# Expert weight splits queued behind the latest hidden-block eviction

## Chip, cores and metric

The kernel runs on one core of a Trainium2 chip. The metric is the device time of one execution in microseconds (us); the figure given for a kernel is the median of several runs.

## The reference

Three stages follow each other: attention with capped scores, a dense two-layer block, and a mixture of eight experts in which every token goes to one expert and every expert takes 224 tokens.

```python
scores = cap * tanh(scale * q @ k.T / cap); attn = softmax(scores)   # 4 x 12 heads, 448 x 64
x = attn @ v                                    # as 1792 tokens x 768
g = relu(x @ w_in) ** 2; x = g @ w_out          # 768 -> 2048 -> 768
logits = x @ w_gate                             # 8 experts
# pairs (token, expert) in falling order of logit; a pair is taken if the
# token is free and the expert has fewer than 1792 / 8 = 224 tokens
for e in range(8):
    out[mask_e] = relu(x[mask_e] @ w1[e]) @ w2[e]   # 768 -> 1024 -> 768, float32
```

## The kernel before

TensorE multiplies in a one-pass 32-bit format that keeps fewer bits than float32. To hold float32 accuracy an operand is split in a high part (a copy in the short format) and a low part (the rest), and three products are summed: high by high, high by low, low by high. For a weight tile of 128 x 768 the split is one copy on ScalarE (L361) and one subtraction on VectorE (L362, called the low half here), in `split_weights`.

The experts run one after the other (`experts`, `expert`). Each has 16 weight tiles, 8 of `w1` and 8 of `w2`, used in that order. This document counts them through: number 16 k + j is tile j of `w1` of expert k, 16 k + 8 + j that of `w2`. In the first half of an expert, block j multiplies the 224 gathered tokens with tile j of `w1` into a PSUM accumulator `acc` (two buffers; in expert 0 some blocks use a `big` one), and is then evicted: ScalarE applies relu and writes the high part (L884), VectorE computes relu again less the high part (L885). The evicted blocks `g` are the stationary operand of the second half, which multiplies them with the tiles of `w2` into two `big` accumulators (L935), copied out (L911) and scattered to the output by POOL (L913). The first four experts multiply their first half in float32 without a split (L867); experts 4 to 7 use split tiles (L874). So 96 of the 128 tiles are split.

A weight tile is loaded by SP's queue (L834) into one of the buffers `wf` (3), `raw` (3) or `g` (6 of a pool of 16), in a pattern that repeats every 12 numbers. `load_experts(n)`, called when tile n is asked for, states loads up to number n + 12 and splits up to number n + 4. The split's results lie in `wh` and `wl`, eight buffers of each in two pools. Before a tile can be loaded the expert that it belongs to must be known: the routing, which picks the experts' tokens with many small VectorE steps (L618 to L768) and small matmuls (L676 to L761), runs beside the experts, and so does the feeding of the next expert: POOL gathers its rows (L783), TensorE transposes them (L802), ScalarE and VectorE split them (L809, L810).

The order of instructions on each engine is fixed when the program is built. On TensorE it is written out. On the other engines a planner plays the program through on an estimated time line: at each point an engine takes, of the instructions that are ready by that estimate, the one of best priority. Priority is the order of statement; `high_priority(5000)` puts the evictions and the feeding ahead of all that is not marked, `high_priority(2000)` the routing. On the chip each engine then works its queue in that order. `issue_after(ins)` gives the planner an edge: the instructions stated in its block on the engine of `ins` take a place behind `ins` in that engine's queue. It adds no wait between engines. Before the change only one such edge concerns the splits: those of expert 0 come behind the latest routing step `self.picks` on VectorE.

Of the kernel before, what the change touches and what calls it, by code (L numbers as in the profile page):

```python
# [9 lines left out]
F32 = mybir.dt.float32  # L10
# [5 lines left out]
AF = mybir.ActivationFunctionType  # L16
OP = mybir.AluOpType
# [14 lines left out]
NF2 = F2 // 128  # L32
# [53 lines left out]
class Kernel:  # L86
# [50 lines left out]
    def second(self, room):  # L137

        self.te, self.late = 0.0, 0
        self.stored = 0  # L140
        self.side = [[0.0, chain(self.last_logits(), self.routes())]]

        def then():
            room()
            yield 0.0

        e = chain(self.output(NB - 1), then(), self.output(LAST), self.experts())
        stuck = False
        while True:
            s = min(self.side, key=lambda x: x[0], default=None)  # L150
            if s is not None and (s[0] <= self.te or stuck):
                stuck = False
                self.te = max(self.te, s[0])
                try:
                    with self.tc.high_priority(2000):
                        wait, pe = next(s[1])
                    s[0] = max(s[0], self.te - 0.5) + wait + pe
                    self.te += pe
                except StopIteration:
                    self.side.remove(s)  # L160
                continue
            try:
                step = next(e)
            except StopIteration:
                return
            stuck = step is None
            self.te += step or 0.0
# [675 lines left out]

    def split_expert(self):
        if len(self.ew[self.eready]) > 1:
            with self.tc.issue_after(self.picks.ins) if self.eready < 2 * NF2 else nullcontext():
                self.ew[self.eready] = self.split_weights(*self.ew[self.eready])

    def expert(self, k):
        nc, ep = self.nc, self.ep  # L850
        xs, idx = self.xe[k], self.rows[k][2]
        hT = []
        W, H = {}, {}

        def part(j, d0, d1):
            if d0 == 0:
                W[j] = [t.rearrange("p (d f) -> p d f", d=ND) for t in self.expert_weights(k, 1, j)]
                if k == 0 and 2 <= j < EARLY:
                    if j % 2 == 0:
                        big = self.psum.tile([128, 2, 512], F32, name="big")  # L860
                        for i in range(2):
                            H[j + i] = big[:, i, :CAP]
                else:
                    H[j] = self.psum.tile([128, CAP], F32, name="acc")
            if k < PLAIN:
                for d in range(d0, d1):
                    nc.tensor.matmul(H[j], W[j][0][:, d], xs[:, d, 0].bitcast(F32), start=(d == 0), stop=(d == ND - 1))  # L867
                    if d % 2:
                        yield 0.8
                return  # L870
            wh, wl = W[j]
            for d in range(d0, d1):
                for w, x, first, last in ((wh, 0, True, False), (wh, 1, False, False), (wl, 0, False, True)):
                    nc.tensor.matmul(H[j], w[:, d], xs[:, d, x], start=(d == 0 and first), stop=(d == ND - 1 and last))  # L874
                if d % 2:
                    yield 0.6

        def evict(j):
            ps = H.pop(j)
            if j % 2 == 0:  # L880
                W["pair"] = self.mp.tile([128, 2, S], F32R, name="g", bufs=NF)
            hT.append(W["pair"][:, j % 2].rearrange("p (a c) -> p a c", a=2))
            with self.tc.high_priority(5000):
                nc.scalar.activation(hT[j][:, 0], ps, AF.Relu)  # L884
                nc.vector.scalar_tensor_tensor(hT[j][:, 1], ps, 0.0, hT[j][:, 0].bitcast(F32), op0=OP.max, op1=OP.subtract)  # L885

        if k == 0:
            for i in range(EARLY):
                p = part(i, 0, DA)
                if i == 0:  # L890
                    yield next(p)
                    yield from self.trailing()
                yield from p
            while self.gathered == 0:
                yield None
            yield from self.feed(0, 1)
        groups = ((0,), (1,), (2, 3), (4, 5), (6,), (7,)) if k == 0 else [(j,) for j in range(NF2)]
        for group in groups:
            for j in group:
                yield from part(j, DA if k == 0 and j < EARLY else 0, ND)  # L900
            for j in group:
                evict(j)
        acc = [self.psum.tile([TP, 2, 512], F32, name="big") for _ in range(2)]
        turned = None

        def store(h):
            if h:
                o = ep.tile([TP, 2, DM // 2], F32, name="o", bufs=1)
            else:
                o = self.mp.tile([128, 2 * S], F32, name="lt", bufs=1)[:TP, :DM].rearrange("p (a b) -> p a b", a=2)  # L910
            nc.scalar.copy(o, acc[h][:, :, :DM // 2])  # L911
            nc.gpsimd.memset(self.spacer, 0.0)
            st = nc.gpsimd.indirect_dma_start(  # L913
                out=self.out, out_offset=bass.IndirectOffsetOnAxis(ap=idx[h][:, :1], axis=0),
                in_=o.rearrange("p a b -> p (a b)"), in_offset=None)
            for s in self.scatters:
                self.tc.declare_no_dep(st.ins, s.ins, reason="rows of other tokens")
            self.scatters.append(st)

        both = [(j, h) for j in range(NF2) for h in range(2)]  # L920
        if k == NE - 1:
            both = both[:NF2] + [(j, h) for h in range(2) for j in range(NF2 // 2, NF2)]
        W2 = {}
        for j, h in both:
            if j >= NF2 // 2 and h == 0 and k + 1 not in self.xe and k + 1 < self.gathered:
                turned = chain(self.feed(k + 1, 0), self.feed(k + 1, 1))
            if j not in W2:
                W2[j] = self.expert_weights(k, 2, j)
            wh, wl = W2[j]
            if turned is not None:  # L930
                yield next(turned, 0.0)
            a, z = (hT[j][:, i, h * TP:(h + 1) * TP] for i in range(2))
            for l, r, first, last in ((a, wh, True, False), (a, wl, False, False), (z, wh, False, True)):
                for s in range(2):
                    nc.tensor.matmul(acc[h][:, s, :DM // 2], l, r[:, s * (DM // 2):(s + 1) * (DM // 2)],  # L935
                                     start=(j == 0 and first), stop=(j == NF2 - 1 and last))
                yield 0.325
            if j == NF2 - 1:
                if h and turned is not None:
                    yield from turned  # L940
                store(h)
        yield 0.5
# [56 lines left out]
```

## Time and profile before

| | |
|---|---|
| median of 3 runs | 1073.3 us (1072.6 to 1077.36) |
| the profiled execution, its own time | 1071.56 us |
| its span, first to last instruction | 1069.8 us |
| TensorE busy | 1034.6 us, 97% |
| VectorE, ScalarE, POOL busy | 604.1, 470.4, 246.6 us |
| mean granted TensorE clock | 0.991 |
| DMA | 237.60 MB, mean 222 GB/s |

Busy time is the time in which an engine had an instruction in work; the ends of matmuls are modelled. A clock of 1.00 is 2.4 GHz and 0.50 is 1.2 GHz. Times in the rows below are counted from the start of the span. In a timeline row the bracket at the end gives the engine's idle time before the instruction and what ended it by the semaphores; no bracket means no idle time worth a note.

### The profile page before, as it was taken

To read this page: it belongs to the slowest core of one execution; us is meant where nothing else is said; L and a number is where in the kernel's file an instruction comes from. 1 tells how busy PE (TensorE), PEld (TensorE's weight loads), DVE (VectorE), ACT (ScalarE), POOL (GpSimd) and SP (SyncE) were. 2 spreads that over 40 slices of the span, in tenths; PEclk is the share of its full clock that TensorE was granted. 3 is DMA by queue.
4 is the path that set the end of the run, shared out by engine and by line. 5 is a ranking of instruction groups with operands and counts; after the bars stand their busy time and mean duration, and the time that the engine had idled before them with its cause. 6 is when DMAs were issued, how large, how long until landed. Compare 5 with 4: busy or idle time off the path is not lost.

```text
span 1069.8 us, 15661 instructions
## 1 busy us (share of the span) xinstructions
PE 1034.6 (97%) x5690; PEld 817.9 (76%) x5690; DVE 604.1 (56%) x1148; ACT 470.4 (44%) x725; POOL 246.6 (23%) x181
## 2 busy tenths in 40 slices
PE   6989999999999999999999999999999999989997
PEld 1335655777777777777888888888899989989997
DVE  5997999998222156566311234453655456666551
ACT  5867686644555633465534110112242233444551
POOL 0117785675221232221000100002220201021000
PEclk8999999999999999999999999999999999999998
DMA  8644777799655589987885368667663539555620
GB/s 277 225 171 134 255 267 261 239 325 334 234 184 182 162 282 348 381 276 272 289 296 192 117 195 278 200 197 231 235 243 133 175 135 321 163 180 185 203 80 27
DMA packets 102495, 237.60 MB, mean 222 GB/s; under 512 B 11089, under 2 KB 21873, under 8 KB 102417
## 3 DMA queue, kind: packets, MB, share of 16 engines
q1 hardware_dynamic: 87776, 219.65, 60.6%
q0 software_dynamic: 3424, 11.19, 3.4%
q10 hardware_dynamic: 11216, 5.75, 2.0%
q8 instruction: 45, 0.74, 0.3%
q14 instruction: 34, 0.27, 0.1%
HBM read 194.08 MB, written 42.47 MB: 221 GB/s over the span
## 4 chain that ended last, share of the span: by engine, by line
PE 67%; issue 13%; DVE 11%; DMA 4%; ACT 2%; POOL 1%; SPq 0%; POOLq 0%; ACTq 0%; DVEq 0%
PE big L935 8%; PE acc L404 7%; PE acc L405 6%; PE acc L406 6%; PE acc L461 6%; PE acc L462 6%; PE acc L463 6%; PE aux L263 4%; PE acc L867 4%; PE big L239 3%; DVE wf L334 3%; DVE wf L333 2%; PE acc L874 2%; PE aux L676 2%; DVE wf L335 1%
## 5 line engine op out<-in xcount | busy, mean ns | idle before, releaser
L461 PE MATMUL acc<-g,wh 128*128 128x448 f32 x384 | 149.5, 389 | 0.0
L404 PE MATMUL acc<-xh,wh 128*128 128x448 f32 x384 | 146.0, 382 | 0.8 <-ACT r L411 0.8
L405 PE MATMUL acc<-xl,wh 128*128 128x448 f32 x384 | 141.2, 368 | 0.5 <-DVE xl L321 0.5
L462 PE MATMUL acc<-g,wh 128*128 128x448 f32 x384 | 140.1, 365 | 0.0
L406 PE MATMUL acc<-xh,wl 128*128 128x448 f32 x384 | 139.9, 364 | 0.0
L463 PE MATMUL acc<-g,wl 128*128 128x448 f32 x384 | 139.6, 364 | 0.0
L935 PE MATMUL big<-wh,g 128*112 128x384 f32 x512 | 118.5, 342 | 1.5 <-DVE g L885 1.5
L243 ACT ACTIVATE p<-big,isc 128x896 f32<-128x896 f32 x96 | 85.8, 907 | 45.0 <-PE big L239 44.2
L272 DVE RECIPROCAL z<-z 128x448 f32<-128x448 f32 x24 | 70.8, 2949 | 57.4 <-ACT z L271 57.3
L416 DVE TENSOR_TENSOR g<-r,g 128x448 fp32r<-128x448 f32 x58 | 42.7, 737 | 104.4 <-ACT g L415 104.1
L404 PEld LDWEIGHTS acc<-xh,wh 128*128 128x128 f32 x384 | 71.6, 187 | 34.2 <-issue 16.3
L244 ACT ACTIVATE p<-p,capt 128x896 f32<-128x896 f32 x96 | 89.3, 948 | 1.7
L783 POOL DMA_INDIRECT xg<-x,idx x32 | 30.8, 964 | 255.4 <-PE aux L676 129.6
L935 PEld LDWEIGHTS big<-wh,g 128*112 128x112 f32 x512 | 86.6, 175 | 2.4 <-DVE g L885 1.8
L461 PEld LDWEIGHTS acc<-g,wh 128*128 128x128 f32 x384 | 73.2, 191 | 11.7 <-issue 5.6
L263 PE MATMUL aux<-p,v 128*64 128x448 f32 x384 | 81.2, 549 | 0.4 <-DVE z L271 0.3
L405 PEld LDWEIGHTS acc<-xl,wh 128*128 128x128 f32 x384 | 72.4, 189 | 10.0 <-DVE xl L321 2.5
L239 PE MATMUL big<-qk 64*128 64x448 f32 x288 | 73.5, 600 | 6.7 <-DMA qk<-qk 6.4
L361 ACT CAST wh<-wf 128x768 fp32r<-128x768 f32 (+1 forms) x64 | 47.9, 751 | 72.9 <-DMA wf<-w 17.3
L411 ACT ACTIVATE r<-acc 128x448 f32<-128x448 f32 x64 | 34.8, 543 | 99.1 <-PE acc L406 87.6
L406 PEld LDWEIGHTS acc<-xh,wl 128*128 128x128 f32 x384 | 72.3, 188 | 6.8 <-issue 0.8
L462 PEld LDWEIGHTS acc<-g,wh 128*128 128x128 f32 x384 | 72.4, 189 | 6.3 <-issue 2.2
(179 smaller groups left out, 1841.2 us busy)
## 6 DMA issues: line engine op xcount, KB each, us to landing
g<-w SPq DMA_DIRECT2D x62, 384.0 KB
wh<-wih SPq DMA_DIRECT2D x48, 384.0 KB
wl<-wil SPq DMA_DIRECT2D x48, 384.0 KB
wh<-woh SPq DMA_DIRECT2D x72, 256.0 KB
wl<-wol SPq DMA_DIRECT2D x72, 256.0 KB
wf<-w SPq DMA_DIRECT2D x33, 384.0 KB
raw<-w SPq DMA_DIRECT2D x33, 384.0 KB
raw<-w_in SPq DMA_DIRECT2D x16, 768.0 KB
```

Source lines behind the costliest of these rows:

```text
L239: nc.tensor.matmul(ps[:, s, :S], k[rows], q[rows], start=True, stop=True)
L243: nc.scalar.activation(p, ps[:, :n, :S], AF.Tanh, scale=self.isc)
L244: e = nc.scalar.activation(p, p, AF.Exp, scale=self.capt)
L263: nc.tensor.matmul(U[hp][s * 64:s * 64 + 64], vt[hp][:, c, s * 64:s * 64 + 64], P[hp, c][:, s if c < KB else 0], start=(c == 0), stop=(c = ...
L272: nc.vector.reciprocal(d, d)
L404: nc.tensor.matmul(ps, wh[:, d], xh, start=(d == 0), stop=False)
L405: nc.tensor.matmul(ps, wh[:, d], xl, start=False, stop=False)
L406: nc.tensor.matmul(ps, wl[:, d], xh, start=False, stop=(d == ND - 1))
L461: nc.tensor.matmul(ps, a, gh, start=(f == 0), stop=False)
L462: nc.tensor.matmul(ps, a, gl, start=False, stop=False)
L463: nc.tensor.matmul(ps, z, gh, start=False, stop=(f == NF - 1))
L935: nc.tensor.matmul(acc[h][:, s, :DM // 2], l, r[:, s * (DM // 2):(s + 1) * (DM // 2)], start=(j == 0 and first), stop=(j == NF2 - 1 and last))
```

## The change

`expert` keeps the two instructions of the eviction stated last in `self.evicts`, and `split_expert` states each split with two more edges: the copy on ScalarE takes a place behind that eviction's ScalarE instruction, the low half behind its VectorE instruction. Until the first eviction of expert 0 is stated there is nothing to come behind. Number, kind and size of the instructions stay as they are.

```diff
@@ second
-        self.stored = 0
+        self.stored, self.evicts = 0, None
@@ split_expert
         if len(self.ew[self.eready]) > 1:
-            with self.tc.issue_after(self.picks.ins) if self.eready < 2 * NF2 else nullcontext():
+            with self.tc.issue_after(self.picks.ins) if self.eready < 2 * NF2 else nullcontext(), self.behind(0), self.behind(1):
                 self.ew[self.eready] = self.split_weights(*self.ew[self.eready])
+
+    def behind(self, i):
+
+        return self.tc.issue_after(self.evicts[i].ins) if self.evicts else nullcontext()
@@ expert, evict
             with self.tc.high_priority(5000):
-                nc.scalar.activation(hT[j][:, 0], ps, AF.Relu)
-                nc.vector.scalar_tensor_tensor(hT[j][:, 1], ps, 0.0, hT[j][:, 0].bitcast(F32), op0=OP.max, op1=OP.subtract)
+                self.evicts = (nc.scalar.activation(hT[j][:, 0], ps, AF.Relu),
+                               nc.vector.scalar_tensor_tensor(hT[j][:, 1], ps, 0.0, hT[j][:, 0].bitcast(F32), op0=OP.max, op1=OP.subtract))
```

## Rows read from the trace of the kernel before

**Rows 1.** The page, busy us (share of the span) xinstructions.

```profile
PE 1034.6 (97%) x5690; PEld 817.9 (76%) x5690; DVE 604.1 (56%) x1148; ACT 470.4 (44%) x725; POOL 246.6 (23%) x181
```

**Rows 2.** Waits of TensorE and ScalarE, 840 to 1070: us in total, times, longest.

```profile
PE acc L867 <- DVE g L885: 2.9, 3, 2.1
...
PE acc L874 <- DVE g L885: 1.6, 4, 0.9
...
ACT wh L361 <- PE acc L874: 33.3, 30, 2.1
```

**Rows 3.** Timeline of TensorE: start, us, instruction, xcount [idle before <-releaser].

```profile
767.88 0.61 PE L935 MATMUL big<-wh,g 128*112 128x384 f32 x2 [1.46 <-DVE g L885]
...
878.10 5.12 PE L867 MATMUL acc<-xs,raw 128*128 128x224 f32 x24 [2.07 <-DVE g L885]
...
892.50 0.68 PE L935 MATMUL big<-wh,g 128*112 128x384 f32 x2
...
912.46 0.46 PE L874 MATMUL acc<-xs,wh 128*128 128x224 f32 x2
...
957.93 0.48 PE L874 MATMUL acc<-xs,wh 128*128 128x224 f32 x2 [2.64 <-issue]
```

**Rows 4.** Timeline of ScalarE.

```profile
764.13 0.83 ACT L361 CAST wh<-wf 128x768 fp32r<-128x768 f32 x1 [1.78 <-DMA wf<-w]
764.87 0.35 ACT L884 ACTIVATE g<-big 128x224 fp32r<-128x224 f32 x1
...
875.78 0.83 ACT L361 CAST wh<-wf 128x768 fp32r<-128x768 f32 x1 [4.00 <-DMA wf<-w]
876.51 0.35 ACT L884 ACTIVATE g<-acc 128x224 fp32r<-128x224 f32 x1
...
914.63 0.84 ACT L361 CAST wh<-wf 128x768 fp32r<-128x768 f32 x1 [0.49 <-PE acc L874]
...
954.40 0.83 ACT L361 CAST wh<-raw 128x768 fp32r<-128x768 f32 x1 [2.89 <-PE aux L709]
955.14 0.35 ACT L884 ACTIVATE g<-acc 128x224 fp32r<-128x224 f32 x1
```

**Rows 5.** Timeline of VectorE.

```profile
876.64 0.96 DVE L362 TENSOR_TENSOR wl<-wf,wh 128x768 fp32r<-128x768 f32 x1 [1.98 <-ACT wh L361]
...
877.66 0.39 DVE L885 SCALAR_TENSOR_TENSOR g<-acc,g 128x224 fp32r<-128x224 f32 x1
...
955.83 0.39 DVE L716 TENSOR_TENSOR A<-aux,room 128x224 bf16<-128x224 f32 x1 [3.06 <-PE acc L874]
956.14 0.38 DVE L718 TENSOR_TENSOR V<-aux,base 128x224 f32<-128x224 f32 x1
956.44 0.27 DVE L717 TENSOR_TENSOR A<-A,tm 128x224 bf16<-128x224 bf16 x1
956.62 0.95 DVE L362 TENSOR_TENSOR wl<-raw,wh 128x768 fp32r<-128x768 f32 x1
957.49 0.39 DVE L885 SCALAR_TENSOR_TENSOR g<-acc,g 128x224 fp32r<-128x224 f32 x1
```

**Rows 6.** Stretches: us, busy PE, PEld, DVE, ACT, POOL, clock, DMA share, GB/s.

```profile
871.00:893.00 22.00, 19.07 (x112) 17.44 (x111) 14.12 (x57) 5.57 (x12) 2.08 (x3) 1.00 0.64 210
893.00:913.00 20.00, 20.00 (x136) 18.86 (x136) 12.32 (x29) 8.64 (x13) 2.20 (x3) 1.00 0.86 304
...
951.00:975.00 24.00, 20.44 (x157) 19.76 (x157) 15.06 (x40) 9.23 (x17) 4.68 (x5) 0.93 0.66 213
```

**Rows 7.** Timeline of SP, loads of weights, merged by buffer kind.

```profile
871.41 6.54 SPq L834 DMA_DIRECT2D wf<-w  x3
...
889.17 1.91 SPq L834 DMA_DIRECT2D wf<-w  x3
```

**Rows 8.** Timeline of VectorE and TensorE, feeding of expert 5.

```profile
942.39 0.60 DVE L810 TENSOR_TENSOR xs<-acc,xs 128x448 fp32r<-128x448 f32 x1
...
943.05 0.60 PE L802 MATMUL acc<-cf,xg 112*128 112x112 f32 x4 [0.17 <-DVE xs L810]
```

## The prediction

> **What bounds the kernel now.** I read four views in this order. First the page's busy times: TensorE is busy 1034.6 us, 97% of the span [rows 1], so a change that leaves the matmuls alone can only take out TensorE's idle time and its time at the lower clock. Before the expert stage (about 740 us) the edited function orders nothing, so the question is how much idle time is left behind that point and what ends it. Second, the waits and the timeline of TensorE: behind 740 us the idle time that ends with an eviction on VectorE (L885, the second half of a hidden block's eviction) is 1.46 us at 767.88 in expert 0, 2.9 us in three waits in expert 3 (the longest, 2.07 us, ends at 878.10) and 1.6 us in four waits in experts 4 to 6; 2.64 us more, which the profile puts down to "issue", end at 957.93 in expert 5 [rows 2, 3]. Third, what stood ahead of these evictions. On ScalarE, expert 3: the split (L361) of a `wf` weight sat at the head of the queue for 4.00 us until its load landed, ran from 875.78 for 0.83 us, and only then came the eviction L884 at 876.51 [rows 4]. On VectorE the low half of that split began at 876.64 and the eviction's half L885 at 877.66, ending 878.05 [rows 5]; TensorE went on at 878.10. So a ready eviction stood behind a split that waited for a load. Expert 0 has the same picture: the split at 764.13 waited 1.78 us for its load, the eviction followed at 764.87 [rows 4]. Fourth, the 2.64 us in expert 5 are no "issue": the engine resumed at 957.93, 0.05 us after the eviction's half that ran 0.39 us from 957.49 [rows 3, 5]. Ahead of that one VectorE worked A (L716, 955.83), two routing steps and a low half (956.62, 0.95 us), and on ScalarE a split at 954.40 stood ahead of the eviction at 955.14 [rows 4, 5].
>
> **The change part by part.** No instruction is added, removed or resized; each split's copy and low half get a place in their queues behind the eviction stated last. Splits are stated four weights ahead of their use but run up to eight ahead now: 30 of them in the stretch behind 840 us wait only until TensorE has released the buffer that they write [rows 2]. That release is the end of a block's matmuls, the very moment at which that block's eviction becomes ready, and the split, stated for a weight eight later, is first in the queue. Behind the change a split stated in block j has to follow the eviction of block j-1, so between two evictions stands the one split stated there and not the one eight ahead; splits stated in the second half of an expert, or in the first block of the next, follow only the last eviction of the expert in work.
>
> Step 1, expert 0: the splits of its second half, numbers 12 to 15, move behind eviction 7, and 10 and 11 behind 5 and 6. The 1.46 us go. What is late next: split 10 is needed by the third weight of the second half, and its copy and low half cost 0.83 + 0.96 us [rows 4, 5], on engines that were idle waiting for that load. Taken as 1.46 gained (bounds 0 and 1.46).
>
> Step 2, expert 3: numbers 60 to 63 move behind the eviction of block 7. All three waits go: 2.9 us. What is late next: the four come due together at the start of the second half, now at 892.50, then about 889.6. Four copies are 3.3 us on ScalarE, four low halves 3.8 us on VectorE. The second half takes 892.50 to 912.46, 20.0 us for eight weights [rows 3], 2.5 each; the first of the four is its fifth weight, 10 us in, so there are 6 us to spare. Cover gone, a late one costs its lateness, at most 3.8 us. VectorE in that stretch is busy 12.3 of 20 us [rows 6]: four low halves come in and three (69 to 71, held behind evictions of expert 4) go out, 13.3. Taken as 2.9 (bounds -0.9 and 2.9).
>
> Step 3, experts 4 to 7, every block: the eviction no longer stands behind 0.83 us of copy and 0.96 us of low half, and has those 1.8 us more until its accumulator is wanted two blocks on. Waits of 1.6 us in four cases are all shorter than 1.8 (the longest 0.9 [rows 2]), so I take the whole 1.6 (bounds 0 and 1.6).
>
> Step 4, expert 5: ScalarE's eviction can run at 954.40 in place of the split. On VectorE A waits for its matmul until 955.83 and I leave it ahead; the eviction follows it directly at about 956.2, in place of two routing steps (0.3 us and 0.2 us, from their starts [rows 5]) and the low half (0.95, overlapping by 0.1). It ends at 956.6 where it ended at 957.87: 1.3 us of the 2.64 go (bounds 0, where A is the true cause, and 2.6, where the eviction passes A too). With it goes clock: the stretch 951 to 975 ran at a granted 0.93 against 1.00 in the two stretches beside it [rows 6]; 0.07 of 24.0 us is 1.7 us, with the engine at the lower of its levels, 1.2 GHz, for a few us right after the 2.64 us idle. After the 2.07 us idle at 878.10 the stretch stayed at 1.00 [rows 3, 6], so I take the shorter idle to keep the clock and count 1.7 (bounds 0 and 1.7). The Trainium skill (TensorE: Matmul & The Clock Gate, section What's actually happening) has the gate follow how busy the engine was lately, with 1.2 GHz after idling; by that rule alone the sum keeps these 1.7 us, and if the low stretch came from something else it would be 7.2 and not 8.9. The row agrees as far as one case can: idle, then low.
>
> Step 5, the loads. A weight's load buffer is free when its split is done, so holding a split back holds the load twelve numbers on, and all behind it in SP's queue, since that works in order. Load 72 goes out at 889.17 [rows 7], and waits now for split 60 at about 890 to 892: 3 us later. Its split ran in ScalarE's queue 25 us later (914.63 [rows 4]), and a load that was waited for took 4.4 us (issued 871.41 [rows 7], split started 875.78 [rows 4]). In the later experts a split moves by at most four weights, some 8 to 10 us, of those 25. Nothing on POOL or ScalarE's queue of transfers is passed. Cost 0; if the cover were gone, a load's lateness.
>
> Step 6, routing and feeding. VectorE's order of routing steps against low halves is drawn anew by the planner, since an edge changes what is ready. Lower bound: the steps in expert 3 come earlier, as the low halves that waited for loads ahead of them are away. Upper: one low half (0.96) in front of a step that TensorE waits for. No row shows one step's wait of that size; the nearest is 0.17 us on a feed step [rows 8]. I take 0.
>
> Sum: 1.46 + 2.9 + 1.6 + 1.3 + 1.7 = 8.9 us. The profiled execution takes 1071.56 us (span 1069.8 and 1.8 around it), so 1062.7 for such a one. The median of the runs shown, 1073.3, is 1.7 above it; taken off that, 1064.4.
>
> **Rivals.** (a) Only the two stages with a late load gain. In expert 5 A keeps its 955.83, the low clock stays, and in experts 4 to 6 the freed place ahead of the eviction is taken by a routing step: 1.46 + 2.9 = 4.4 us, 1068.9. For it: A's wait until 955.83 has nothing to do with a split, and the 1.6 us are sums of 0.2 to 0.9. Against: the eviction in those blocks has the highest priority of what is ready.
> (b) The change does not bite: the splits that hold the engine up would be ones that the edges do not reach, because they were stated behind an older eviction. By the statement order, numbers 60 to 63 are stated in the second half of expert 3, behind its last eviction, so this needs an error of mine in the counting: 1073.3.
> (c) Slower: the low halves crowd the feeding of the next expert. Held back, they fall in the second half of experts 3 to 6, where three pairs of transposes (L802) each wait for a subtraction (L810) to release the accumulator. That chain has no slack today: the third transposes waited 0.17 us for the subtraction that began at 942.39 [rows 8]. With one more low half ahead of each of 3 subtractions, 0.96 us each, in 4 experts: 11.5 us lost against 8.9 gained, 1073.3 + 2.6 = 1075.9. It decides as soon as ten of the twelve feeds are hit. Against: the subtraction has the eviction's priority, and the backlog of four low halves is worked off in the first 4 us of a stretch whose feeding starts halfway.
>
> **How the numbers follow.** About 0.5% (5.4 us) is what a measurement of this kernel can tell from no change. The sum as worked has 0.56, with its own range 1060 to 1067.9; (a) 0.28, (b) 0.05, (c) 0.11. The forecast is 1064.4. Its lower end adds the upper bound of step 4 (1.3 more) and a lucky routing order of some 3 us, 1060; the upper end takes in (a) and reaches to no change, 1073; only (c) and single misses stay outside. Faster than 1067.9: 0.56. Within 5.4 us: (a) and (b) and a mild form of (c), 0.35. Slower: 0.09.
>
> **What would show it.** In the changed kernel ScalarE's timeline should show L884 ahead of each L361 that follows the same block's matmuls, no L361 with a wait for a load between two L884 of experts 0 and 3, and TensorE's waits for L885 behind 740 us should fall from 6.0 us (1.46 + 2.9 + 1.6) to under 1. The stretch of expert 5's first half should be at 1.00. Step 4 is wrong if the gap there remains over 2 us; step 5 if an L361 of experts 4 to 7 waits for a load; step 6 if waits for L810 or for routing steps come up. The forecast as a whole is wrong if TensorE's idle time falls as said and the span does not follow it.

## The result, and the profile after

The changed kernel takes 1056.25 us (median of five runs, 1056.15 to 1058.11) where the kernel before takes 1072.6 (five runs, 1072.0 to 1077.36): a ratio of 0.9841, 95% interval 0.9816 to 0.9866. The 16.4 us gained are nearly twice the 8.9 forecast, and the time lies below the range of 1060 to 1073. The profiled execution after takes 1056.75 us (span 1055.0), 14.8 less than that of before; the other 1.5 are where the two profiled executions lie about their medians (before 1.0 below, after 0.5 above).

In the code after, line numbers behind the edges are four higher: the eviction is L888 and L889, the matmuls of the experts are L871, L878 and L939, the copy out is L915.

The page after, busy us by engine, beside [rows 1]: TensorE is 8.1 us shorter at work, though it has the same 5690 matmuls; the mean granted clock is 0.997 where it was 0.991.

```profile
PE 1026.5 (97%) x5690; PEld 815.2 (77%) x5690; DVE 602.5 (57%) x1148; ACT 468.1 (44%) x725; POOL 244.7 (23%) x181
```

The waits after, 830 to 1056 us (total, times, longest), beside [rows 2]: TensorE's 2.9 and 1.6 us for the eviction's VectorE half are down to 0.2 and 0.5, and the row of 33.3 us in which ScalarE's splits waited for a block of a first half (L874, now L878) is gone; splits still wait for second halves (L939).

```profile
ACT wh L361 <- PE big L939: 12.3, 14, 1.4
...
ACT wh L361 <- DMA raw<-w: 1.3, 1, 1.3
...
PE acc L878 <- DVE g L889: 0.5, 1, 0.5
PE acc L871 <- DVE g L889: 0.2, 1, 0.2
```

TensorE's timeline after, at the places of [rows 3]. Expert 0's second half begins without a wait (764.76), expert 3's first half runs through (872.80), its second half begins at 885.43 and ends at 905.43, and of expert 5's gap 1.48 us are left.

```profile
764.76 0.68 PE L939 MATMUL big<-wh,g 128*112 128x384 f32 x2
...
872.80 6.97 PE L871 MATMUL acc<-xs,raw 128*128 128x224 f32 x36
...
885.43 0.67 PE L939 MATMUL big<-wh,g 128*112 128x384 f32 x2
...
905.43 0.46 PE L878 MATMUL acc<-xs,wh 128*128 128x224 f32 x2
...
948.45 0.48 PE L878 MATMUL acc<-xs,wh 128*128 128x224 f32 x2 [1.48 <-issue]
```

ScalarE after, at the places of [rows 4]: the eviction L888 now stands ahead of the copy L361, in expert 3 and in expert 5.

```profile
875.27 0.36 ACT L888 ACTIVATE g<-acc 128x224 fp32r<-128x224 f32 x1 [1.91 <-PE acc L871]
875.52 0.82 ACT L361 CAST wh<-g 128x768 fp32r<-128x768 f32 x1
...
946.00 0.36 ACT L888 ACTIVATE g<-acc 128x224 fp32r<-128x224 f32 x1 [3.54 <-PE aux L709]
946.26 0.82 ACT L361 CAST wh<-wf 128x768 fp32r<-128x768 f32 x1
```

The stretches after (first and second half of expert 3, first half of expert 5), beside [rows 6]: TensorE is busy throughout expert 3, and the clock in expert 5 is 1.00.

```profile
864.00:886.00 22.00, 22.00 (x134) 21.64 (x134) 15.22 (x60) 7.20 (x14) 4.01 (x4) 1.00 0.64 197
886.00:906.00 20.00, 20.00 (x136) 18.85 (x135) 13.96 (x32) 9.77 (x15) 3.30 (x4) 1.00 0.97 326
942.00:966.00 24.00, 21.99 (x193) 21.38 (x193) 17.16 (x45) 11.93 (x21) 5.31 (x6) 1.00 0.75 235
```

TensorE's order is the same in both kernels, so the n-th matmul of one answers to the n-th of the other, and the difference of their starts tells by stage where time was gained. The traces of the kernel before and of the changed kernel shown so far are called the first pair; a second pair was profiled later on one chip (the last experiment below). In us:

| | forecast | first pair | second pair |
|---|---|---|---|
| up to the first transposes that feed expert 0 | 0 | 1.78 | 0.51 |
| from there to the start of expert 0 | 0 | -0.83 | 1.63 |
| expert 0 | 1.46 | 2.10 | 0.64 |
| experts 1 and 2 | 0 | 0.03 | 1.13 |
| expert 3 | 2.9 | 3.95 | 4.12 |
| expert 4 | 0.36 | 1.29 | 1.31 |
| expert 5 | 0.89 + 1.3 + 1.7 | 4.13 | 2.02 |
| expert 6 | 0.32 | 1.31 | 1.08 |
| expert 7 | 0 | 1.06 | 1.07 |
| up to the last matmul | 8.9 | 14.82 | 13.51 |

The first row is no work of the change: up to there ScalarE, VectorE and POOL work the same order in both kernels, and the two traces of the kernel before differ by 1.17 us at the same place (740.34 and 739.17). From there on both pairs gain 13.0 us.

### The profile page after: what moved, and what is told of

Its sections match the earlier page's. It is cut to its first block, busy times and chain, and to the rows that moved or that the text cites. A ratio compares the mean times of both kernels' runs of the same rounds, so it can differ in the third digit from the quotient of the medians.

```text
span 1055.0 us, 15657 instructions
## 1 busy us (share of the span) xinstructions
PE 1026.5 (97%) x5690; PEld 815.2 (77%) x5690; DVE 602.5 (57%) x1148; ACT 468.1 (44%) x725; POOL 244.7 (23%) x181
## 4 chain that ended last, share of the span: by engine, by line
PE 71%; issue 12%; DVE 10%; DMA 3%; ACT 1%; POOL 1%; SPq 0%; POOLq 0%; ACTq 0%; DVEq 0%
PE big L939 8%; PE acc L404 7%; PE acc L405 6%; PE acc L406 6%; PE acc L461 6%; PE acc L871 6%; PE acc L462 6%; PE acc L463 6%; PE aux L263 4%; PE big L239 3%; DVE wf L334 3%; DVE wf L333 2%; PE acc L878 2%; PE aux L676 2%; PE aux L269 1%
## 5 line engine op out<-in xcount | busy, mean ns | idle before, releaser
L939 PE MATMUL big<-wh,g 128*112 128x384 f32 x512 | 118.5, 343 | 0.0
L939 PEld LDWEIGHTS big<-wh,g 128*112 128x112 f32 x512 | 86.7, 175 | 0.7
L463 PEld LDWEIGHTS acc<-g,wl 128*128 128x128 f32 x384 | 72.0, 187 | 6.7 <-issue 0.7
```

The costliest lines, as they stand in the source:

```text
L463: nc.tensor.matmul(ps, z, gh, start=False, stop=(f == NF - 1))
```

## The experiments

The theory was that of the prediction: the gain comes from evictions that no longer stand behind a split, at three kinds of place (a late load in experts 0 and 3, every block of experts 4 to 7, routing step A in expert 5). The rivals were that one engine's edge does all the work, that the edges matter through the loads or the feeding, and that the gain of expert 5 belongs to the chip and not to the queues. The runs were taken in three groups on three chips, and each ratio below is to runs of the kernel before in the same group: 1073.02 us in the first (edges for one half, product order, eight ahead), 1069.18 in the second (VectorE's edge, both parts together, the change again), 1069.45 in the third. Times expected for the second group were reckoned from the level of the first pair and the first group, and are some 4 us high.

**Edges for one half of the experts each.** The edges are put only on splits of experts 0 to 3, and only on those of experts 4 to 7.

```diff
-        return self.tc.issue_after(self.evicts[i].ins) if self.evicts else nullcontext()
+        return self.tc.issue_after(self.evicts[i].ins) if self.evicts and self.eready < 2 * NF2 * PLAIN else nullcontext()
```

The other kernel has `>=` in place of `<`.

> The new edges only for the splits of experts 0 to 3 (numbers below 64). Theory (an eviction that stands behind a split in ScalarE's queue holds up TensorE; the two kinds of standing behind, for a late load in experts 0 and 3 and for a buffer's release in experts 4 to 7, add up): the trace of the change gave 2.2 us at expert 0 and 3.8 us in expert 3, so 6 us faster than the kernel before, near 1066.5, with the first halves of experts 4 to 7 as before. Rival (what counts is how far ahead splits and loads run in the later experts, paced by the edges): almost nothing, 1071 or more. Rival (the planner's new order of routing steps did it): no number; experts 4 to 7 would change too.

> The new edges only for the splits of experts 4 to 7 (numbers from 64 on). Theory: the rest of the gain, 8 to 10 us, near 1063.5, with the waits of experts 0 and 3 as before (1.5 us at the start of expert 0's second half, 2.9 us in expert 3). The two parts together should give the whole 16 us within 1.5 us. Rival (pacing): the whole gain, 1057.

Measured: 1064.86 us (0.9926, 0.9896 to 0.9957) and 1068.64 (0.9944, 0.992 to 0.9969), beside 1073.02 for the kernel before. Against the first trace of before, the early edges give 1.25 us in expert 0, 3.99 in the first half of expert 3 and 1.2 in all of experts 4 to 7 (1.0 of it in expert 5, where the clock stayed at 1.00); the late edges give nothing in experts 0 to 3, where all waits stay, and 7.8 us in experts 4 to 7, as in the changed kernel. So by stage the two halves act apart, and the late one is the larger: 7.8 us, where the prediction's terms for it sum to 4.6 (1.6 + 1.3 + 1.7). By the medians they do not add up as expected: 8.2 and 4.4 us make 12.5, not 16 within 1.5, and the late-edge kernel is 5 us above the 1063.5 expected. Its profiled execution lost 3.9 us in expert 0 against the first trace of before, and shows what the early edges remove, worse than there: in expert 0 an eviction stood behind two copies, the first of which waited for its load, and TensorE waited 2.26 us. ScalarE, then TensorE, then the stretch behind it:

```profile
767.57 0.83 ACT L361 CAST wh<-wf 128x768 fp32r<-128x768 f32 x1 [1.24 <-DMA wf<-w]
768.48 0.83 ACT L361 CAST wh<-raw 128x768 fp32r<-128x768 f32 x1
769.22 0.35 ACT L888 ACTIVATE g<-big 128x224 fp32r<-128x224 f32 x1
...
770.05 0.78 PE L939 MATMUL big<-wh,g 128*112 128x384 f32 x2 [2.26 <-DVE g L889]
...
770.00:777.00 7.00, 6.95 (x38) 6.10 (x39) 4.32 (x15) 0.31 (x2) 0.00 (x0) 0.52 0.80 313
```

**The VectorE edge alone.** Which of the two edges carries the gain in experts 4 to 7?

```diff
-nullcontext(), self.behind(0), self.behind(1):
+nullcontext(), self.behind(1):
```

> Only the edge on VectorE, none on ScalarE. ScalarE's queue then keeps the splits' copies ahead of the evictions in experts 4 to 7 and, for late loads, in expert 3. Theory (ScalarE's queue decides, since VectorE's half of an eviction cannot start before ScalarE's): at most the 2 us of expert 0, 1069 to 1073; the waits of expert 3 and the 1.1 to 1.3 us each in experts 6 and 7 stay. Rival (the low halves on VectorE are the costly part, 0.96 us against 0.83): half the gain or more, 1064 or less.

Measured: 1060.73 us (0.9918, 0.989 to 0.9946). My expectation (1069 to 1073) fell, and the rival (1064 or less) held: the first halves of experts 4, 6 and 7 gain 0.9, 1.3 and 1.1 us, all that the change gives there, although on ScalarE the copy still stands ahead of the eviction. ScalarE, then VectorE, in expert 6:

```profile
987.64 0.83 ACT L361 CAST wh<-g 128x768 fp32r<-128x768 f32 x1 [0.36 <-PE acc L878]
988.38 0.35 ACT L888 ACTIVATE g<-acc 128x224 fp32r<-128x224 f32 x1
...
990.39 0.35 ACT L888 ACTIVATE g<-acc 128x224 fp32r<-128x224 f32 x1
...
988.76 0.39 DVE L889 SCALAR_TENSOR_TENSOR g<-acc,g 128x224 fp32r<-128x224 f32 x1 [7.29 <-ACT g L888]
989.07 0.95 DVE L362 TENSOR_TENSOR wl<-raw,wh 128x768 fp32r<-128x768 f32 x1
```

The eviction goes straight from ScalarE to VectorE, and blocks follow each other at 2.01 us (988.38, 990.39). With a copy (0.83) and a low half (0.96) ahead of it the eviction is too late; without the low half it is in time. Whether it would be in time without the copy alone is not shown: with ScalarE's edge alone the planner builds the same program, instruction for instruction, as with both, so ScalarE's edge already brings VectorE's order with it. In expert 3, where the copy waits for a load, VectorE's edge can't help: waits of 1.25 and 0.67 us stay there (877.38, 880.59). Its second half then loses 1.06 us: a low half that waits for a late copy (897.65) stands ahead of a routing step (L684, 898.52), and TensorE waits for that. This is the upper bound that step 6 of the prediction named and found in no row. In the traces this kernel stays 9.5 us short of the change on the same chip, 3.9 of it ahead of expert 0 and 3.8 in expert 3.

```profile
898.73 0.16 PE L687 MATMUL aux<-votes,unit 128*128 128x1 bf16 x1 [0.90 <-DVE votes L684]
```

**The product order turned.** Why does a split come ahead of an eviction at all? In the kernel before, the last product of a block reads `wl`, so the tile's `wh` buffer is free one matmul before the accumulator is done (the prediction had both at the very same moment), and the planner takes the split that waits for this buffer first. Here the products with `wh` come last; there are no edges.

```diff
-                for w, x, first, last in ((wh, 0, True, False), (wh, 1, False, False), (wl, 0, False, True)):
+                for w, x, first, last in ((wl, 0, True, False), (wh, 0, False, False), (wh, 1, False, True)):
```

> The kernel before, without any of the new edges; only the order of the three products in the first halves of experts 4 to 7 is turned: low by high first, high by high, high by low last. The high part's buffer is then free with the last matmul of a block and not one matmul earlier, so split and eviction become ready at the same moment and the eviction's priority decides; splits still run eight ahead. Theory (who stands first at the end of a block is all): the gain of experts 4 to 7 comes without the edges, 7 to 9 us, near 1064.5; experts 0 and 3 as before. Rival (the gain needs the splits and loads held back): no gain, 1072.

Measured: 1066.84 us (0.9929, 0.9909 to 0.9949). Against the first trace of before, experts 4 to 7 gain 7.3 us of the 7.8 that the change gains there, and experts 0 and 3 nothing; the medians differ by 6.2, a little under the 7 to 9 expected. So in the late experts nearly all that the change does is to put the eviction ahead of a split that was ready one matmul earlier.

**The early edges with the turned products.** Both parts together, without an edge on the late experts.

```diff
+        return self.tc.issue_after(self.evicts[i].ins) if self.evicts and self.eready < 2 * NF2 * PLAIN else nullcontext()
...
-                for w, x, first, last in ((wh, 0, True, False), (wh, 1, False, False), (wl, 0, False, True)):
+                for w, x, first, last in ((wl, 0, True, False), (wh, 0, False, False), (wh, 1, False, True)):
```

> Edges for the splits of experts 0 to 3 alone, and in experts 4 to 7, in place of the edges, the turned order of the three products (low by high first). Theory (two separate causes, and each is taken away by any means that puts the eviction first): the same as the change, 1056 to 1058.5. Rival (the edges do something in experts 4 to 7 that the turned order does not, such as later loads): short of the change by 3 us or more, 1060.

Measured: 1054.85 us (0.9864, 0.9837 to 0.9892), beside 1052.97 (0.9853, 0.9827 to 0.9879) for the change on the same chip. The two causes are the whole of the gain to within 1.9 us; the version is no better than the change.

**Splits stated eight ahead.** The edges stay, but a split is stated eight weights before its use, so the eviction it follows is an older one.

```diff
-            while self.eready < min(n + 5, self.eloaded):
+            while self.eready < min(n + 9, self.eloaded):
...
-        while self.eready < min(n + 5, self.eloaded):
+        while self.eready < min(n + 9, self.eloaded):
```

> The change with all its edges, but splits are stated eight weights ahead of their use and not four. A split is still behind the latest eviction stated, but in experts 4 to 7 the one stated in block j needs the buffer that block j releases, so it stands in ScalarE's queue ahead of the eviction of block j again. Theory: the gain of experts 4 to 7 is lost, that of experts 0 and 3 mostly kept: 1064 to 1068. Rival (it is enough that splits come behind an eviction, or that the planner drew a new order): 1056 to 1058. Rival (pacing): 1070 or more.

Measured: 1063.59 us (0.9907, 0.9875 to 0.9939), 0.4 under the range expected. Expert 3 keeps its 3.99 us; experts 4, 6 and 7 lose theirs (0, 0.2 and 0 left). An edge to an older eviction leaves the split ahead of the current one: the edge works through where it puts the split, as rival (b) of the prediction would have had it in the change itself.

**The change again, and routing step A behind the eviction.** A second trace of the change, and beside it a kernel in which A (L716) of expert 5 follows the eviction of block 0 on VectorE, to see whether what is left of the gap is A's place.

```diff
-        v.tensor_tensor(A, p4, over(self.room), op=OP.is_lt)
+        with self.behind(1): v.tensor_tensor(A, p4, over(self.room), op=OP.is_lt)
...
-                if d % 2:
+                if d % 2 and d < ND - 1:
...
-                evict(j)
+                evict(j), (yield 0.6) if k >= PLAIN else None
```

> The changed kernel as it is, to compare the next ones with on the same chip. Both theories: 1056 to 1057, with waits of 1.5 and 0.5 us in the first half of expert 5 as the only ones left behind 760 us that are over 0.3.

> The changed kernel with one swap: in expert 5 the eviction of block 0 stands ahead of the routing step A (L716) in VectorE's queue, and A behind it. All other queues stay as they are. Theory (what is left there is the same thing once more, an eviction behind an instruction that waits): both waits go, 1.5 to 2 us faster than the changed kernel, near 1054.5. Rival (TensorE's finish of a block is reported late there, while POOL issues scatters and gathers, and holds up whatever comes next): the wait moves to the eviction of block 1 and stays over 1 us; no difference that counts, 1055.5 to 1057.

Measured: 1052.97 us (0.9853, 0.9827 to 0.9879) and 1054.74 (0.9861, 0.9836 to 0.9887); 1056 to 1057 was expected for the change. On this chip the change had no wait at all in expert 5, where 1.48 and 0.53 us were expected, so A's place could not be tested: the first half of expert 5 is equal in both to 0.01 us. What did show is that the gap is not the kernel's alone.

**Both kernels on one chip.** The kernel before, the change, and the kernel with A moved, each unaltered.

> The kernel before once more, so that it and the change are profiled on one chip (the first pair of traces may come from two). In question is the gap in the first half of expert 5: 2.64 us in the kernel before, 1.48 us in the first trace of the change, none in its second trace. Theory 1 (the queues): before has the gap on every chip, because the copy and the low half stand ahead of the eviction there; then the first half of expert 5 gains 3 to 4 us against the change on this chip, and the whole difference is 15 to 17 us. Theory 2 (late signals of the chip): the gap is there only where instructions that wait for TensorE start over 1 us behind the modelled end of their matmuls; then, if this chip shows no such lag, before has under 1 us of idle time there, the half gains about 1.5 us like the first halves of experts 6 and 7, and the whole difference is 13 to 14 us.

> The change beside it. Both theories: the gains by stage of the first pair in experts 0 (1.3 to 2.2), 3 (about 4.0), 4 (0.9), 6 (1.3) and 7 (1.1), against the kernel before of this chip. Theory 1: expert 5's first half 3 to 4. Theory 2: 1.5 without the lag; with it, a gap of 1 to 1.5 us is seen in the change as well.

> The changed kernel with routing step A (L716) of expert 5 put behind the eviction of the first block in VectorE's queue, as in the run before, on a chip that may show the lag. Theory 1 (what is left of the gap in the change is A's place): where the change beside it has a gap of 1 to 1.5 us there, this one has under 0.5, and is 1 to 2 us faster. Theory 2 (the late signal itself is the gap): the gap stays within 0.4 us of that of the change. If the change shows no gap on this chip, both expect no difference over 0.5 us in that half.

Measured: 1067.32 us for the kernel before (0.9988, 0.9975 to 1.0001, of the 1069.45 that the same kernel takes in the other runs of this group), 1055.56 for the change (0.9872, 0.9844 to 0.9899), 1055.2 with A moved (0.987, 0.9845 to 0.9895). Theory 2 held: here the kernel before itself has no gap, only 0.22 and 0.85 us of idle time in expert 5's first half, that half gains 2.0 us, not 3.6, and the whole difference of the two traces is 13.5 (11.8 by these medians, 13.9 against 1069.45). A's place stays untested. What differs is when the engines that wait for TensorE start. In the first trace of before, block 0's last matmul starts at 952.79 and ends by the model at 953.07, and ScalarE's copy that waits for that block starts at 954.40 [rows 4], 1.33 us behind; block 1's last ends at 955.29 by the model, and the copy behind it starts at 958.81, 3.5 us late. In the second trace block 0's last matmul starts at 954.77, and the copy at 954.97, before the modelled end. TensorE and ScalarE, first trace:

```profile
952.79 0.28 PE L874 MATMUL acc<-xs,wl 128*128 128x224 f32 x1
...
958.81 0.83 ACT L361 CAST wh<-raw 128x768 fp32r<-128x768 f32 x1 [3.33 <-remote]
```

And the second trace, with the stretch 951 to 975 at a clock of 1.00 where the first had 0.93 [rows 6]:

```profile
954.77 0.28 PE L874 MATMUL acc<-xs,wl 128*128 128x224 f32 x1
...
954.97 0.83 ACT L361 CAST wh<-raw 128x768 fp32r<-128x768 f32 x1 [1.48 <-PE acc L874]
...
951.00:975.00 24.00, 22.82 (x200) 21.86 (x199) 16.82 (x45) 11.81 (x20) 6.31 (x6) 1.00 0.76 237
```

## Why the prediction was wrong

The direction, the mechanism and, but for one, the places were right; the size was not. The signs that it named came: TensorE's waits for the eviction behind 740 us fell from 6.0 to 0.7 us, and the stretch of expert 5's first half is at 1.00. The step that failed first is step 3 ("Waits of 1.6 us in four cases"): its term was 1.6 us and measured 5.1 to 5.3. The same fault, a wait read where it shows only in part, is in steps 1 and 2 as well. In all, 8.9 us were forecast and 13.0 gained from the feeding of expert 0 on.

**Step 3: 1.6 us forecast, 5.1 to 5.3 measured** (experts 4 to 7, with expert 5's 2.0 of the second pair and without 0.4 us of feeding in expert 4). I summed TensorE's idle time at matmuls. The same waits stand at the weight loads ahead of them, and are longer there. The waits of weight loads (PEld) for the eviction in the first trace of before, behind 740 us:

```profile
PEld acc L867 <- DVE g L885: 5.0, 6, 2.4
PEld acc L874 <- DVE g L885: 3.6, 9, 1.1
...
PEld big L935 <- DVE g L885: 1.8, 1, 1.8
```

That is 10.4 us, against 2.9 + 1.6 + 1.5 = 6.0 at the matmuls. In the second trace of before these rows read 5.7, 4.1 and 1.3, 11.1 us in all; in the second trace of the change none of them is left, and the second pair gained 11.4 from expert 0 on. By stage the two agree to about 0.3 us, over and under, once the waits for a gather and the feeding are taken off: 4.4 us of such waits and 4.1 gained in expert 3, 0.85 and 1.07 in expert 6. One such wait in expert 6, weight load first, then the matmuls around it:

```profile
1001.75 0.30 PEld L874 LDWEIGHTS acc<-xs,wh 128*128 128x128 f32 x2 [0.28 <-DVE g L885]
...
1001.15 0.39 PE L874 MATMUL acc<-xs,wh 128*128 128x224 f32 x2
1001.38 0.28 PE L874 MATMUL acc<-xs,wl 128*128 128x224 f32 x1
1001.75 0.48 PE L874 MATMUL acc<-xs,wh 128*128 128x224 f32 x2
```

The row of the matmuls at 1001.75 has no bracket. The matmul before it is drawn from 1001.38 to 1001.66, and the 0.09 us up to 1001.75 are too short to be noted. But matmuls of this kind start 0.11 to 0.12 us apart (two from 1001.15, the third at 1001.38), so the next was due at about 1001.49: 0.26 us are lost, and 0.17 of them lie under the drawn end of the one before. The Trainium skill says that such ends are estimated and not observed (Perfetto Trace Analysis, section Tensor Engine Instruction); these rows agree, and show what it costs a reader who counts idle time at matmuls.

The same can be read from the blocks' pace. ScalarE's evictions in expert 6 before, then after:

```profile
995.93 0.35 ACT L884 ACTIVATE g<-acc 128x224 fp32r<-128x224 f32 x1
...
1000.31 0.35 ACT L884 ACTIVATE g<-acc 128x224 fp32r<-128x224 f32 x1
...
1004.68 0.35 ACT L884 ACTIVATE g<-acc 128x224 fp32r<-128x224 f32 x1
```

```profile
984.64 0.36 ACT L888 ACTIVATE g<-acc 128x224 fp32r<-128x224 f32 x1 [0.93 <-PE acc L878]
...
986.65 0.36 ACT L888 ACTIVATE g<-acc 128x224 fp32r<-128x224 f32 x1 [0.93 <-PE acc L878]
...
988.66 0.36 ACT L888 ACTIVATE g<-acc 128x224 fp32r<-128x224 f32 x1 [0.93 <-PE acc L878]
```

Two blocks take 4.38 and 4.37 us before, 4.02 after: 0.36 us a pair, three pairs an expert, 1.1 us. The first halves gain 1.1 to 1.3 in experts 6 and 7 and 0.9 in expert 4. Expert 7, which I put at nothing, gains 1.06 and 1.07, expert 6 1.31 and 1.08.

**Step 2: 2.9 forecast, 4.0 and 4.1 measured**, for the same reason: the weight loads of that half waited 4.3 us in four cases. What I named as late next cost nothing: its second half takes 20.0 us as before (885.43 to 905.43), with VectorE busy 13.96 us (13.3 reckoned).

**Step 1: 1.46 forecast, 2.1 and 0.6 measured.** The weight load's wait was 1.8 us in the first trace and 1.3 in the second. The rest is mostly a wait for a gather while expert 0 is fed: 0.44 us before and none after in the first pair, 0.93 and 1.43 in the second. Taken off, the step gives 1.7 and 1.1. The 1.1 us of expert 1 in the second pair are of the same kind: there one eviction stood behind a copy that had waited 2.71 us for its load, the next behind a second copy, and TensorE waited 0.71.

**A step that I did not see** lies ahead of expert 0. Splits of its second half were run before its first half had begun, three of them ahead of the copy that feeds it (L807), and each waited for a load. Numbers 8 and 9 are stated before there is an eviction to follow and stay; number 10 moves behind eviction 5, as step 1 says, and so out of the feeding, which step 1 did not say. ScalarE in the second pair, before and then after:

```profile
740.58 0.83 ACT L361 CAST wh<-g 128x768 fp32r<-128x768 f32 x1 [7.50 <-DMA g<-w]
741.66 0.83 ACT L361 CAST wh<-g 128x768 fp32r<-128x768 f32 x1 [0.24 <-DMA g<-w]
742.74 0.83 ACT L361 CAST wh<-g 128x768 fp32r<-128x768 f32 x1 [0.25 <-DMA g<-w]
743.47 0.53 ACT L807 COPY xs<-aux 128x448 f32<-128x448 f32 x1
```

```profile
739.51 0.83 ACT L361 CAST wh<-g 128x768 fp32r<-128x768 f32 x1 [6.91 <-DMA g<-w]
740.59 0.83 ACT L361 CAST wh<-g 128x768 fp32r<-128x768 f32 x1 [0.25 <-DMA g<-w]
741.33 0.53 ACT L807 COPY xs<-aux 128x448 f32<-128x448 f32 x1
```

The feeding copy stands behind two loads in place of three, and these land 1.08 us apart; the other 1.07 of the 2.14 us is that the first load came earlier in this run. In the second pair TensorE's wait for the feeding copy falls from 2.62 to 0.99 us. In the first pair the copy is 0.96 us earlier (742.23 to 741.27), and expert 0 starts 0.95 earlier; but TensorE had come to the feeding 1.78 earlier, and its wait rose from 0.20 to 1.03, since the loads came no sooner. Of the thirteen profiles, three copies stand ahead in the six whose early splits have no ScalarE edge or are stated eight ahead, and the feeding copy starts at 742.19 to 743.52; in the seven others two stand ahead, and it starts at 739.88 to 742.00.

**Step 4: 3.0 forecast, 2.1 in the first pair, none in the second.** In the first pair expert 5 gains 4.13 us, 2.0 of which the second pair has too. Of the other 2.1, the clock's 1.7 came about as reckoned (the stretch is at 1.00), by luck more than by rule. The gap itself shrank by 1.2 us, but a wait of 0.53 stands behind it now (951.25). VectorE after, beside [rows 5]: A starts as late as before behind its matmuls, and the eviction follows two instructions later.

```profile
947.41 0.39 DVE L716 TENSOR_TENSOR A<-aux,room 128x224 bf16<-128x224 f32 x1 [4.18 <-PE acc L878]
947.72 0.38 DVE L718 TENSOR_TENSOR V<-aux,base 128x224 f32<-128x224 f32 x1
948.01 0.38 DVE L889 SCALAR_TENSOR_TENSOR g<-acc,g 128x224 fp32r<-128x224 f32 x1
```

The step took a disturbance that other chips don't show for a property of the kernel. That a shorter idle time keeps the clock was no more than a guess; the last section has a longer one (2.62 us) at full clock and a shorter one (2.24) with a fall.

**Steps 5 and 6: nothing forecast, nothing lost.** The next three loads behind expert 3's first half go out 2.5 us after the start of its second half (887.89) where they went 3.3 before it [rows 3, 7], 5.8 us later and not 3, and no eviction waits for them. One row of the waits after has a copy of experts 4 to 7 wait for a load, 1.3 us (the `raw` row above), which step 5 named as its sign of being wrong. But that copy (1005.12, in the second half of expert 6) is of number 115, which came into a `g` buffer by one of six loads issued from 985.26 to 988.72, and the copy ahead of it (1003.01) waited the same 1.26 us for a matmul (L939). So that its load held it up is not shown, and no wait of TensorE follows. The feeding of expert 5 no longer waits ([rows 8] had 0.17 us), and the second half of expert 4 gains 0.4 us: rival (c) went the other way there. Before, a low half (941.52) ran right ahead of the subtraction at 942.39; after, none does. Of all twelve feeding subtractions five still have a low half right ahead of them, where six had, and TensorE waits for none.

Rival (a), "only the two stages with a late load gain", fell with the kernel whose edges reach experts 4 to 7 alone (7.8 us there).

## What to carry to other kernels

Read a TensorE wait at its weight load, not at its matmul, and check it by the pace of equal blocks: waits of 0.3 us that no matmul row shows, one every second block, gave experts 6 and 7 about 1.1 us each, where the matmul rows had 0.32 and 0. Where a list scheduler sets the order of a queue, look for work that becomes ready an instant before more urgent work; and count every instruction that an edge takes out of an earlier stage, not only those of the stage in view. Profile before and after on one chip before a stage's wait is put down to the code.

## What the runs showed of the hardware

The engines that wait for TensorE can start late. In expert 5 ScalarE started 1.24 to 1.33 us behind the modelled end of block 0 in both traces of the first pair and in three of the four kernels measured together next, and 3.4 to 3.6 us behind that of block 1 (after: 950.41 against 946.98). With splits stated eight ahead it is within 0.3 us for these two blocks, and 2.26 us behind that of block 2 (954.12 against 951.86). In all seven traces of the two other groups, each on a chip of its own, it started within 0.1 us behind blocks 0 and 1. POOL issues the same six scatters and gathers, 0.9 to 1.6 us each, beside it in both, so that work alone doesn't explain it. The cause is open.

The clock does not follow from one idle time. With the edges on experts 0 to 3 alone, expert 5 had 2.62 us of idle time and stayed at 1.00; with splits stated eight ahead, 2.24 us at the same place and 0.93 over 24 us; with the edges on experts 4 to 7 alone, 2.26 us in expert 0 and 0.52 over the 7 us behind it. The first two, the gap and the stretch:

```profile
951.45 0.48 PE L878 MATMUL acc<-xs,wh 128*128 128x224 f32 x2 [2.62 <-issue]
...
944.00:968.00 24.00, 19.39 (x165) 18.60 (x164) 15.15 (x41) 9.77 (x18) 5.18 (x6) 1.00 0.70 215
```

```profile
956.60 0.77 PE L878 MATMUL acc<-xs,wh 128*128 128x224 f32 x2 [2.24 <-DVE g L889]
...
944.00:968.00 24.00, 21.40 (x173) 20.59 (x173) 15.18 (x41) 10.14 (x18) 5.68 (x6) 0.93 0.69 223
```

The Trainium skill (TensorE: Matmul & The Clock Gate, section What's actually happening) has the gate go by how busy the engine was lately. These rows don't settle that: over the 24 us TensorE ran more matmuls in the stretch that fell (173, busy 21.40 us) than in the one that kept 1.00 (165, busy 19.39 us). They do show that the length of one wait doesn't tell which way the clock goes.
